# Products of ones in TensorE's planned waits, new prices and new ranks for a planned order: block-causal attention with a gated feed-forward on one core

## Chip, core and metric

The kernel runs on one core of a Trainium2 chip. The metric is the device time of one execution in microseconds (us), as a median over runs.

## What is computed

Attention over 8 batches and 8 heads (576 positions, head size 64) with a mask by blocks of 64 positions, and then a gated feed-forward layer over all 4608 rows, in fp32. The inputs of the feed-forward weights are in 64-bit floats.

```python
scores = scale * np.matmul(q, k.transpose(0, 1, 3, 2))
scores = np.where(block_i >= block_j, scores, -1000000000.0)
scores = scores - np.max(scores, axis=-1, keepdims=True)
attn = np.exp(scores)
attn = attn / (np.sum(attn, axis=-1, keepdims=True) + 1e-09)
attn_out = np.matmul(attn, v)
x = attn_out.transpose(0, 2, 1, 3).reshape(B * S, H * D)    # 4608 x 512
g = x @ w_gate                                               # 512 x 1536
val = x @ w_val
out = (g * (1.0 / (1.0 + np.exp(-g))) * val) @ w_out         # 1536 x 512
```

## The kernel before

The program first makes a list of tasks, and no task issues an instruction at that point. A task has an engine, a cost in us, a rank, a function that issues its instructions, the tasks that it waits for, and the buffers that it uses (`add`, `dma`). `in_order` (L1288) then plays the list on a clock of its own: whenever an engine is free, it takes the ready task with the lowest rank for which the buffers are free, and adds its cost. The order of the tasks that comes out is the order in which the functions are called (L1382 to L1385), and so each engine's program order. The chip then runs each engine in that order, held by semaphores alone. What a cost or rank changes is therefore the order, never the work.

The tasks are these.

- Attention goes by pairs of heads. For batches 0 and 1 (`FIRST`, stretches of 0 to 256 and 256 to 576 positions) `plain_scores` loads q and k (L387), turns them on TensorE (L411) into PSUM, copies them out with ScalarE (L419), makes the scores (L437, fp32), and ScalarE copies them to `sc` (L455) and hides the masked blocks (L469), which reads the scores' PSUM buffer last. Batches 2 to 7 split q and k into a high and a low fp32r part (`row_scores`, products L648; `split_scores`, products L564). Then VectorE takes the maximum over chunks (L705), GpSimd over partitions (L709), VectorE subtracts it (L733), ScalarE takes the exponent (L737), and TensorE multiplies with `v` (L777); in batch 0 it also multiplies with `ones` there for the sums. Later the sums are taken by TensorE (L836, L843, batch 1) or by GpSimd (L828).
- A piece of a weight (`weight`, 12 pieces of three weights) is loaded as 64-bit words (L944), brought to fp32 by ScalarE (L959, L963) and VectorE (L968, L973), and split into a high part (L978) and a low one (L981). The loads hang in one chain, and five `wo` buffers hold them. Their ranks are in `PIECES`, those of some first loads in `AHEAD`.
- The feed-forward goes by 18 tiles of 256 rows (`feed_forward`): the products with the gate and value weights into `gv` (L1100 to L1102, three fp32r products of 256 columns for each part of the depth), tanh (L1133), two operations of VectorE (L1136, L1141), the split of the result (L1146, L1149), and the products with the third weight into `po` (L1191 to L1193). Tiles 0 and 1 take their ranks from `SIDE`, later ones from their place; attention of batch b has the rank 10 + b - `LEAD`, and its scores `EAGER` less.

PSUM is held by five buffers: two `at`, two `gv` and one `po`. A task that writes one has to wait until the last reader of what stood there is done. `ones` is a 128 x 64 tile of 1.0, set by VectorE's first instruction.

Of the kernel before, what the change touches and what calls it, by code (L numbers as in the profile page):

```python
# [18 lines left out]
def kernel(  # L19
# [33 lines left out]
    LEAD, EAGER = 1.69311, 0.3  # L53
# [85 lines left out]
    class Task:  # L139
        def __init__(self, engine, cost, rank, fn, after, bufs, port, mode):  # L140
            self.engine, self.cost, self.rank, self.fn = engine, cost, rank, fn
            self.bufs, self.waits, self.next, self.ready = bufs, 0, [], 0.0
            self.moves, self.port, self.mode = 0.0, port, mode

            self.prev = None
# [3 lines left out]
    def add(engine, cost, rank, fn, after=(), bufs=(), port=False, mode=""):  # L149
# [9 lines left out]
        t.n = len(tasks)  # L159
        tasks.append(t)  # L160
        return t
# [8 lines left out]
    def mm_us(*ns):  # L170
        return sum(n / 2400.0 + 0.0145 for n in ns)
# [170 lines left out]
    def attention(R, b, h, a, e, early, bufs, lane):  # L342
# [35 lines left out]
        def plain_scores():  # L378
# [21 lines left out]
            for i in range(2):  # L400
# [24 lines left out]
                tr = add("PE", 0.083 * nb, R, transposes, [ld[i]], [qk, ps, prt])  # L425
                ready.append(add("ACT", act_us(nb * TB, True), R, out_of_psum, [tr], [ps, prt]))

            for visit in visits:
# [19 lines left out]
                for parts, ps in zip(visit, both):  # L448
# [25 lines left out]
                    if whole:  # L474
# [9 lines left out]
                        t = add("ACT", act_us(4 * BLK) + 0.1, Q, hide_there, [pr], [ps])  # L484
                        t = add("ACT", act_us(2 * W), Q, max_there, [t], [ps, mx])
# [4 lines left out]
                    if mixed:  # L490
                        t = add("ACT", 0.245 * len(mixed), Q, hide, [t], [ps, sc])
                    if parts[0][:2] == (0, 0):
                        t = add("ACT", 0.46, Q, first_max, [t], [ps, sc, mx])
# [3 lines left out]
        def split_scores():  # L497
# [48 lines left out]
            for x in range(2):  # L546
                for group in (((0, 0, half), (0, half, half)), ((1, 4), (2, 3))):
# [40 lines left out]
                    us = mm_us(*(w for _, _, w, _, _ in parts)) * 2  # L588
                    pr = add("PE", us, Q, products, ready[x], [ps, high, prt[x], sc])
# [123 lines left out]
        for c in (1, *later):  # L713
            ms.append(
                add(
                    "DVE",
                    dve_us(2 * (e - first[c])),
                    Q,
                    lambda c=c: merged(c, mx, ALU.max, scores_of),
                    [*evac[0], *evac[c], *ms[0:1], *ms[-1:]],  # L720
                    [*stays, sc, mx],
                    not stays,
                )
            )
        mm = [add("POOL", 0.1 + W * 0.0034, Q, lambda x=x: max_all(x), ms, [mx]) for x in range(2)]
# [149 lines left out]
        elif by_pe:  # L875
            tot = Buf("at", also=banks)
            sm = add("PE", pair_us(W), R, sum_all, ss, [sc, su, tot], mode="columns")
            sm = [add("ACT", act_us(W) + 0.1, R, sums_out, [sm], [tot, sr])] * 2
            total = lambda x0, x1: sr[0][x0 * D : x1 * D : D, :]
        else:  # L880
            assert (a, e) == (0, S)
            ss.append(add("ACT", act_us(2 * P), R, sum_first, [exps[0], *taken], [sc, su]))
            sm = [add("POOL", 3.82, R, lambda x=x: reduced(x), ss, [su]) for x in range(2)]
# [126 lines left out]
    def bring_x(j, t0, w):  # L1010
# [31 lines left out]
        for d in range(NDC):  # L1042
# [18 lines left out]
            m = dma(R, 2e5, r_load, [a], [rt], 2)  # L1061
# [4 lines left out]
    def feed_forward(j, t0, w, xs):  # L1066
# [19 lines left out]
        def up(i, which, prev):  # L1086
# [3 lines left out]
            for y in range(2):  # L1090

                for ds in [range(NDC)] if j >= FINE else [[d] for d in range(NDC)]:

                    def products(ds=ds, y=y):
# [11 lines left out]
                        mm_us(w, w, w) * len(ds),  # L1106
# [3 lines left out]
                        [ps, *(xs[d][1] for d in ds)],  # L1110
                    )
# [5 lines left out]
        for i in range(0, NFC, 2):  # L1117
# [65 lines left out]
            for piece in pieces:  # L1183
# [14 lines left out]
                t = add("PE", mm_us(DM, DM, DM) * len(piece), rank(i), products, after, bufs)  # L1198
# [45 lines left out]
    add("ACT", 1.4, 2.01, lambda: nc.scalar.activation(seen, seen, AF.Exp))  # L1244
# [43 lines left out]
    def in_order():  # L1288
# [4 lines left out]
        engines = ("PE", "DVE", "ACT", "POOL", "SP")  # L1293
# [4 lines left out]
        events = [0.0]  # L1298
# [32 lines left out]
        while events:  # L1331
# [3 lines left out]
            for e in engines:  # L1335
# [22 lines left out]
                if e == "PE":  # L1358
                    end, mode, last = end + 0.2 * (t.mode != mode), t.mode, t
# [21 lines left out]

    order = in_order()  # L1382
    with tc.manual_schedule():
        for t in order:
            t.fn()  # L1385
# [28 lines left out]
```

## Time and profile before

| | |
|---|---|
| median of 3 runs | 1177.16 us |
| lowest and highest run | 1176.88 and 1179.21 us |
| span of the profiled execution, first to last instruction | 1173.6 us |
| TensorE busy | 1145.5 us, 98% of the span |
| VectorE, ScalarE, GpSimd busy | 758.9, 620.4, 325.5 us |

The span is the profiled execution's own time; the median of the runs is 3.6 us above it. The page divides the span into busy time by engine; further views give the busy time in stretches, what each engine waited for, groups of instructions by line, and the instructions in order of time. TensorE's weight loads are counted apart and overlap with its products. A product's recorded end is modelled, and neighbours overlap in the record, so how long a group takes is read from the start of the next. The granted clock is given as a share of 2.4 GHz.

### The profile page before, as it was taken

The page shows a single profiled execution, that of the slowest core. Times are in us where ns is not written, and L with a number is a line of the kernel's source. Part 1 is how long each engine was busy: PE and PEld are TensorE (multiplying, and loading weights), DVE is VectorE, ACT ScalarE, POOL GpSimd, SP SyncE. Part 2 cuts the span into 40 slices and gives each one's busy share as a digit, 9 for nine tenths or more (in the row PEclk, how much of TensorE's full clock was granted, in tenths as well). Part 3 has the DMA queues.
Part 4 walks back from the last instruction along what each step waited for, and adds up shares of the span by engine and source line. Part 5 has one row for each costly group of instructions (what it writes and reads, how often), then busy time and mean ns, then how long its engine had stood idle before and what let it go on. Part 6 is the DMA issues. An engine that isn't in the chain of part 4 may idle for free.

```text
span 1173.6 us, 21780 instructions
## 1 busy us (share of the span) xinstructions
PE 1145.5 (98%) x8512; PEld 1024.7 (87%) x8512; DVE 758.9 (65%) x1230; ACT 620.4 (53%) x1114; POOL 325.5 (28%) x139
## 2 busy tenths in 40 slices
PE   5889999999999999999999999999999999999998
PEld 4568778898898989988998899898989899999997
DVE  6988988575887668768575859575767533323222
ACT  6978876546573837465656555555646312212111
POOL 3222100144535251434444334252432500000000
PEclk9989999999999999999999999999999999999999
DMA  8658756766564756656565565655663445444432
GB/s 225 188 151 219 201 187 226 206 178 166 169 148 137 198 164 167 195 166 168 152 188 160 152 177 163 187 146 161 164 202 108 145 148 197 140 167 136 143 134 100
DMA packets 266982, 197.40 MB, mean 168 GB/s; under 512 B 195264, under 2 KB 231376, under 8 KB 266880
## 3 DMA queue, kind: packets, MB, share of 16 engines
q1 hardware_dynamic: 264304, 195.29, 56.9%
q8 instruction: 67, 1.10, 0.4%
q10 hardware_dynamic: 2576, 0.72, 0.3%
q14 instruction: 35, 0.29, 0.1%
HBM read 171.57 MB, written 24.38 MB: 167 GB/s over the span
## 4 chain that ended last, share of the span: by engine, by line
PE 85%; DVE 5%; ACT 4%; DMA 3%; issue 1%; POOL 1%; SPq 1%; ACTq 0%; DVEq 0%; POOLq 0%
PE gv L1100 16%; PE gv L1102 15%; PE gv L1101 15%; PE po L1191 7%; PE po L1193 7%; PE po L1192 7%; PE at L777 7%; PE at L564 6%; DVE sc L733 1%; DVE mx L705 1%; DMA wo<-in_moe_w_val_dram 1%; POOL mx L709 1%; DMA wo<-in_moe_w_out_dram 1%; ACT ob L959 1%; PE at L648 1%
## 5 line engine op out<-in xcount | busy, mean ns | idle before, releaser
L709 POOL PARTITION_ALL_REDUCE mx<-mx x80 | 144.1, 1850 | 408.7 <-issue 135.2
L1100 PE MATMUL gv<-xhl,v_all 128*128 128x256 f32 x864 | 241.8, 280 | 0.8 <-DVE t L1136 0.7
L1102 PE MATMUL gv<-xhl,v_all 128*128 128x256 f32 x864 | 239.7, 277 | 0.0
L1101 PE MATMUL gv<-xhl,v_all 128*128 128x256 f32 x864 | 239.3, 277 | 0.0
L828 POOL PARTITION_ALL_REDUCE mx<-mx x48 | 178.9, 3775 | 201.4 <-DVE mx L705 192.8
L1136 DVE SCALAR_TENSOR_TENSOR t<-t,gv 128x512 f32<-128x512 f32 x108 | 74.0, 685 | 215.4 <-ACT t L1133 215.2
L1100 PEld LDWEIGHTS gv<-xhl,v_all 128*128 128x128 f32 x864 | 162.1, 188 | 4.9 <-issue 2.5
L1101 PEld LDWEIGHTS gv<-xhl,v_all 128*128 128x128 f32 x864 | 162.3, 188 | 0.6
L1102 PEld LDWEIGHTS gv<-xhl,v_all 128*128 128x128 f32 x864 | 162.2, 188 | 0.2
L1133 ACT ACTIVATE t<-gv 128x512 f32<-128x512 f32 x108 | 64.6, 598 | 171.2 <-PE gv L1102 171.1
L1191 PE MATMUL po<-wo,hhl 128*128 128x512 f32 x372 | 147.7, 397 | 0.0
L1192 PE MATMUL po<-wo,hhl 128*128 128x512 f32 x372 | 145.6, 391 | 0.0
L1193 PE MATMUL po<-wo,hhl 128*128 128x512 f32 x372 | 145.1, 390 | 0.2 <-DVE hhl L1149 0.2
L1146 ACT CAST hhl<-t 128x512 fp32r<-128x512 f32 x108 | 67.0, 620 | 132.1 <-DVE t L1141 129.7
L733 DVE TENSOR_TENSOR sc<-sc,mx 128x640 f32<-128x640 f32 (+6 forms) x168 | 122.7, 765 | 11.7 <-POOL mx L709 11.6
L737 ACT ACTIVATE sc<-sc 128x1024 f32<-128x1024 f32 (+3 forms) x104 | 106.0, 1029 | 45.3 <-DVE sc L733 44.9
L1100 PE MATMUL gv<-xhl,g_even 128*128 128x256 f32 x432 | 123.7, 286 | 0.0
L1102 PE MATMUL gv<-xhl,g_even 128*128 128x256 f32 x432 | 122.2, 283 | 0.4 <-DVE g_even L981 0.4
L1101 PE MATMUL gv<-xhl,g_even 128*128 128x256 f32 x432 | 122.1, 283 | 0.0
L1100 PE MATMUL gv<-xhl,g_odd 128*128 128x256 f32 x432 | 120.7, 279 | 0.0
L1101 PE MATMUL gv<-xhl,g_odd 128*128 128x256 f32 x432 | 119.6, 277 | 0.0
L1102 PE MATMUL gv<-xhl,g_odd 128*128 128x256 f32 x432 | 119.6, 277 | 0.0
(171 smaller groups left out, 2368.8 us busy)
## 6 DMA issues: line engine op xcount, KB each, us to landing
wo<-wo_d SPq DMA_DIRECT2D x200, 512.0 KB
out_dram<-ob SPq DMA_DIRECT2D x35, 256.0 KB
v<-in_v_dram SPq DMA_DIRECT2D x64, 128.0 KB
xt<-x_d SPq DMA_DIRECT2D x64, 128.0 KB
rt<-r_d SPq DMA_DIRECT2D x128, 64.0 KB
qk<-in_q_dram SPq DMA_DIRECT2D x112, 72.0 KB
qk<-in_k_dram SPq DMA_DIRECT2D x104, 72.0 KB
x_d<-xu SPq DMA_DIRECT2D x24, 288.0 KB
```

The costliest lines, as they stand in the source:

```text
L709: nc.gpsimd.partition_all_reduce(m, m, channels=P, reduce_op=bass_isa.ReduceOp.max)
L733: nc.vector.tensor_tensor(piece(c), scores_of(c), m, ALU.subtract)
L737: nc.scalar.activation(x, x, AF.Exp)
L777: nc.tensor.matmul(ps[0][own(x), 1 - i if sums else i, q0 - s0 : s1 - s0], lhsT=ones if sums else vt[0][:, 2 * lane + c, own(x)], rhs=sc[0 ...
L828: nc.gpsimd.partition_all_reduce(m, m, channels=P, reduce_op=bass_isa.ReduceOp.add)
L1100: nc.tensor.matmul(o, lhsT=hi[:, d], rhs=xhi[:, 0:w], start=first, stop=False)
L1101: nc.tensor.matmul(o, lhsT=hi[:, d], rhs=xlo[:, 0:w], start=False, stop=False)
L1102: nc.tensor.matmul(o, lhsT=lo[:, d], rhs=xhi[:, 0:w], start=False, stop=last)
L1136: nc.vector.scalar_tensor_tensor(t[0][:, 0:n], t[0][:, 0:n], 1.0, pg[0][:, 0:n], ALU.add, ALU.mult)
L1191: nc.tensor.matmul(po, lhsT=hi, rhs=whi, start=i + y == 0, stop=False)
L1192: nc.tensor.matmul(po, lhsT=hi, rhs=wlo, start=False, stop=False)
L1193: nc.tensor.matmul(po, lhsT=lo, rhs=whi, start=False, stop=i + y == NFC - 1)
```

## The change

It has four parts.

1. `keep_busy`: where the list leaves TensorE idle for over 0.3 us ahead of a task, and this task is the first user of an `at`, `gv` or `po` buffer, products of `ones` with `ones` (64 columns, into a corner of that buffer) are issued ahead of the task: one per 0.25 us of the planned gap if the task is planned before 8 us, else `FILL` (0.6) of the gap at one per 0.12 us. The task's own first product starts the buffer anew, so nothing of them is left.
2. Prices: products of the feed-forward (`up_us`, `down_us` in place of `mm_us`), a table `CHANGE` for going from one kind of product to another in place of 0.2 us, double time for TensorE before 7 us (`WARM`), GpSimd's reductions, transfers (`moves`, and 1.1 us instead of 0.9 us from the queue to the landing, 1.0 us more for `r_load`), and some small operations of ScalarE and VectorE.
3. Rules: the engines are served in another order, GpSimd takes no new task while VectorE is at a task marked `port`, and `PATIENCE` goes from 10 to 42.3 us.
4. All ranks are new: `LEAD`, `EAGER`, `AHEAD`, `LATER`, `PIECES`, `SIDE`, `FIRST`, and the lead times `spare`.

The diff without the hunks that only hand on a new price or the name of a stage:

```diff
@@ -50,7 +50,7 @@
     XT = 256
 
 
-    LEAD, EAGER = 1.69311, 0.3
+    LEAD, EAGER = 6.2781, 3.1665
 
     SUMS = 2
 
...
@@ -60,31 +60,32 @@
 
     FINE = 4
 
-    AHEAD = {(0, 1): 2.01, (0, 2): 2.07, (1, 0): 2.03, (1, 1): 2.5, (1, 2): 2.5}
-    LATER = 0.6
+    AHEAD = {(0, 1): 22.5417, (0, 2): -10.3365, (1, 0): 8.2032, (1, 1): -19.9721, (1, 2): 6.7332}
+    LATER = 2.3757
 
     PIECES = [
-        (2.46498, 1.85126, 2.0295),
-        (4.86232, 5.94853, 3.63137),
-        (4.59615, 2.52017, 1.48427),
-        (3.86967, 3.05824, 5.34888),
-        (1.93206, 3.59139, 2.41171),
-        (5.13877, 6.90631, 5.83015),
-        (3.57653, 2.93377, 2.93471),
-        (0.0797053, 1.36382, 0.915695),
-        (-2.09572, -5.85789, -4.34371),
-        (-7.47749, -5.87222, -3.82425),
-        (-7.64215, -9.14061, -8.44419),
-        (-12.1092, -9.50108, -10.8836),
+        (-6.5049, -13.4704, 10.7146),
+        (14.0963, 21.3025, 1.4141),
+        (32.0858, -0.6456, 5.5541),
+        (8.9744, 6.387, 21.8701),
+        (-12.6217, 6.2755, -24.5098),
+        (28.2796, 26.9596, 9.5596),
+        (13.4146, 37.4905, 9.0606),
+        (-36.2639, -18.6986, -5.0973),
+        (-0.5887, -7.6401, -28.1413),
+        (-6.5449, -1.352, -10.4626),
+        (-29.8841, -4.8378, -26.6713),
+        (-13.3057, -19.018, -13.6853),
     ]
 
-    SIDE = (2.97811, 4.18833)
-
-    PATIENCE = 10.0
+    SIDE = (-30.4952, 24.7881)
+
+    PATIENCE = 42.3358
+    FILL = 0.6
 
     FIRST = {
-        0: [(0, 256, (-4.21445, 2.40818, 2.05548, 2.12375)), (256, 576, (-2.9124, -2.06995, -6.61901, -4.10645))],
-        1: [(0, 256, (4.0214, 3.93624, 4.15916, 3.63076)), (256, 576, (-2.93177, 1.89587, 2.55533, 4.50202))],
+        0: [(0, 256, (-37.8906, -5.2559, -7.864, 5.3255)), (256, 576, (-14.6577, -11.0435, -35.6463, 0.7383))],
+        1: [(0, 256, (11.6297, 16.6813, 14.7013, -5.4466)), (256, 576, (-3.4185, 3.2769, 6.4793, 1.1216))],
     }
     TILES = [XT] * (NT // XT)
 
...
@@ -167,17 +168,21 @@
     def dve_us(n, one=False):
         return 0.07 + n * (0.00052 if one else 0.00104)
 
-    def mm_us(*ns):
-        return sum(n / 2400.0 + 0.0145 for n in ns)
+    def up_us(n):
+        return n * 0.1134 + (0.012 if n < 3 * NDC else 0.0)
+
+    def down_us(n):
+        return n * 0.2267
 
 
     def pair_us(*ns):
         return sum(n / 600.0 + 0.01 for n in ns)
 
-    def dma(rank, size, fn, after=(), bufs=(), n=1, engine="SP", packet=1024):
+    def dma(rank, size, fn, after=(), bufs=(), n=1, engine="SP", packet=1024, late=0.0):
 
         t = add(engine, 0.5 * n, rank, fn, after, bufs)
-        t.moves = size / packet * (9.0 + 0.0385 * packet) / 16e3
+        t.moves = size / packet * (9.5 + 0.0405 * packet) / 16e3
+        t.late = 1.1 + late
         return t
 
 
...
@@ -722,7 +727,7 @@
                     not stays,
                 )
             )
-        mm = [add("POOL", 0.1 + W * 0.0034, Q, lambda x=x: max_all(x), ms, [mx]) for x in range(2)]
+        mm = [add("POOL", 0.33 + W * 0.0028, Q, lambda x=x: max_all(x), ms, [mx]) for x in range(2)]
 
 
         exps, taken = {}, []
...
@@ -1290,20 +1296,31 @@
 
         import heapq
 
-        engines = ("PE", "DVE", "ACT", "POOL", "SP")
+        engines = ("PE", "POOL", "DVE", "ACT", "SP")
         idle = {e: 0.0 for e in engines}
         could = {e: [] for e in engines}
         room = {tag: [(0.0, i) for i in range(len(s))] for tag, s in slots.items()}
         turn = dict.fromkeys(slots, 0)
-        events = [0.0]
+        events = [0.6]
         for t in tasks:
             if not t.waits:
                 could[t.engine].append(t)
         order = []
         now = queue = 0.0
-        mode, last = "", None
-
-        spare = {"PE": 2.11536, "DVE": 0.315845, "ACT": 0.745908, "POOL": 0.0, "SP": 0.0}
+        mode, last, stage, two = "", None, "", False
+
+        WARM = 7.0
+        CHANGE = {
+            "": {"columns": 0.1, "rows": 0.2},
+            "up": {"down": 0.02, "split": 0.01, "columns": 0.13, "rows": 0.2},
+            "down": {"up": 0.072, "split": 0.01, "columns": 0.13, "rows": 0.2},
+            "split": {"up": 0.072, "down": 0.05, "columns": 0.13, "rows": 0.2},
+            "columns": {"up": 0.195, "down": 0.2, "split": 0.2, "rows": 0.19, "turn": 0.15},
+            "rows": {"up": 0.195, "down": 0.2, "split": 0.2, "columns": 0.13, "rows": 0.04, "turn": 0.15},
+            "turn": {"up": 0.04, "down": 0.04, "split": 0.04, "columns": 0.13, "rows": 0.2},
+        }
+
+        spare = {"PE": 1.9535, "DVE": 0.3392, "ACT": 0.7494, "POOL": 0.0, "SP": 0.0}
 
         def place(t, by):
 
...
@@ -1343,6 +1360,8 @@
                 )
                 if e == "DVE" and idle["POOL"] > now:
                     cand = [t for t in cand if not t.port]
+                if e == "POOL" and idle["DVE"] > now and two:
+                    continue
 
                 follow = [(now, t) for t in cand if t.prev is not None and t.prev is last]
                 if any(t.ready < now - PATIENCE for t in cand):
...
@@ -1356,13 +1375,19 @@
                 order.append(t)
                 end = now + t.cost
                 if e == "PE":
-                    end, mode, last = end + 0.2 * (t.mode != mode), t.mode, t
+                    key = t.mode or t.stage
+                    end, mode, last, stage = end + CHANGE[stage].get(key, 0.0), t.mode, t, key
+                    t.gap, t.at = now - max(idle[e], 0.6), now
+                    if now < WARM:
+                        end += end - now
+                if e == "DVE":
+                    two = t.port
                 idle[e] = end
                 heapq.heappush(events, end)
                 done = end + (0.2 if e == "PE" else 0.13)
                 if t.moves:
                     queue = max(queue, end + 0.65) + t.moves
-                    done = queue + 0.9
+                    done = queue + t.late
                 heapq.heappush(events, done)
                 for u in t.bufs:
                     u.left -= 1
...
@@ -1379,9 +1404,25 @@
         assert len(order) == len(tasks), (len(order), len(tasks), [(t.engine, t.rank, t.fn.__qualname__) for t in left][:10])
         return order
 
+    def keep_busy(t):
+        for u in t.bufs:
+            if u.tag in ("at", "gv", "po") and t is first_user[u]:
+                break
+        else:
+            return
+        to = u[0] if u.tag == "gv" else u[0][:, 0]
+        for _ in range(int(t.gap / 0.25 if t.at < 8.0 else FILL * t.gap / 0.12)):
+            nc.tensor.matmul(to[0:D, 0:D], lhsT=ones, rhs=ones, start=True, stop=True)
+
     order = in_order()
+    first_user = {}
+    for t in order:
+        for u in t.bufs:
+            first_user.setdefault(u, t)
     with tc.manual_schedule():
         for t in order:
+            if t.engine == "PE" and t.gap > 0.3:
+                keep_busy(t)
             t.fn()
 
 
```

## Rows read from the trace of the kernel before

**Rows 1.** The page, part 1: busy us (share of the span), instructions.

```profile
PE 1145.5 (98%) x8512; PEld 1024.7 (87%) x8512; DVE 758.9 (65%) x1230; ACT 620.4 (53%) x1114; POOL 325.5 (28%) x139
```

**Rows 2.** Busy time by stretch: us, busy us (instructions) of each engine, clock, DMA.

```profile
0.00:80.00 80.00, 59.29 (x462) 42.40 (x463) 64.25 (x142) 61.12 (x120) 22.44 (x26) 0.96 0.71 187
80.00:260.00 180.00, 176.70 (x1305) 147.83 (x1304) 146.16 (x249) 128.34 (x227) 36.05 (x23) 1.00 0.70 203
...
360.00:1160.00 800.00, 800.00 (x5918) 736.76 (x5917) 470.72 (x724) 367.69 (x659) 220.08 (x75) 1.00 0.54 160
1160.00:1173.60 13.60, 9.81 (x63) 8.50 (x61) 2.49 (x4) 2.18 (x4) 0.00 (x0) 0.94 0.21 75
```

**Rows 3.** TensorE's waits up to 80 us: who waited for whom, us, times, longest.

```profile
PE gv L411 <- DVE ident L316: 4.4, 1, 4.4
PE at L437 <- ACT sc L469: 3.6, 3, 1.6
PE po L437 <- ACT sc L469: 2.1, 1, 2.1
...
PE at L777 <- ACT parts L419: 1.3, 1, 1.3
PE at L437 <- DVE xt L811: 1.2, 1, 1.2
PE at L777 <- ACT sc L469: 1.1, 1, 1.1
```

**Rows 4.** Busy time by stretch, three of 10 us and one of 2 us.

```profile
10.00:20.00 10.00, 7.68 (x54) 6.09 (x54) 5.82 (x14) 8.68 (x18) 5.90 (x6) 1.00 0.95 244
20.00:30.00 10.00, 6.00 (x51) 4.15 (x51) 9.69 (x21) 7.70 (x15) 2.48 (x2) 1.00 0.86 244
30.00:40.00 10.00, 7.32 (x71) 5.18 (x67) 9.55 (x22) 9.40 (x18) 2.76 (x2) 1.00 0.66 162
...
68.00:70.00 2.00, 2.00 (x10) 0.95 (x8) 2.00 (x5) 1.57 (x4) 0.00 (x0) 0.50 0.79 210
```

**Rows 5.** The split of the weights (L981): durations ns, first and last start us.

```profile
L981 DVE TENSOR_TENSOR v_all<-wo,v_all x14: 650/685/694, 25.4 to 197.2; 128x512 fp32r<-128x512 f32 x14
```

**Rows 6.** TensorE in order of time, 55 to 74 us: start, us, operation, xcount, idle before.

```profile
55.70 2.27 PE L777 MATMUL po<-sc,v 128*64 128x320 f32 x20
57.80 2.23 PE L777 MATMUL po<-sc,ones 128*64 128x320 f32 x20
...
67.03 4.32 PE L777 MATMUL at<-sc,v 128*64 128x320 f32 x20 [1.11 <-ACT sc L469]
71.13 3.10 PE L777 MATMUL at<-sc,ones 128*64 128x320 f32 x20
```

**Rows 7.** TensorE in order of time to 21 us.

```profile
8.78 2.44 PE L411 MATMUL gv<-ident,qk 96*128 96x96 f32 x12 [0.97 <-DMA qk<-in_q_dram]
...
11.15 1.65 PE L437 MATMUL at<-parts,parts 64*128 64x256 f32 x8
12.59 1.49 PE L437 MATMUL po<-parts,parts 64*128 64x256 f32 x8
14.01 1.11 PE L411 MATMUL gv<-ident,qk 96*128 96x96 f32 x6
...
18.97 0.71 PE L411 MATMUL at<-ident,qk 96*128 96x96 f32 x6 [0.74 <-DVE sc L733]
20.43 0.92 PE L437 MATMUL at<-parts,parts 64*128 64x256 f32 x8 [0.74 <-ACT parts L419]
```

**Rows 8.** Groups of VectorE by line: busy us, mean ns of one.

```profile
L1149 DVE TENSOR_TENSOR hhl<-t,hhl 128x512 fp32r<-128x512 f32 x108 | 93.1, 862 | 40.8 <-ACT hhl L1146 40.0
L1136 DVE SCALAR_TENSOR_TENSOR t<-t,gv 128x512 f32<-128x512 f32 x108 | 74.0, 685 | 215.4 <-ACT t L1133 215.2
```

**Rows 9.** ScalarE and TensorE in order of time, around 264 us.

```profile
262.65 1.06 ACT L737 ACTIVATE sc<-sc 128x1024 f32<-128x1024 f32 x1
...
265.08 1.68 PE L777 MATMUL at<-sc,v 128*64 128x256 f32 x14
```

More of the change, by code (lines that the diff above doesn't have):

```diff
@@ L143, in __init__, with add @@
             self.moves, self.port, self.mode = 0.0, port, mode
-            self.prev = None
+            self.prev, self.stage = None, ""
     tasks = []
-    def add(engine, cost, rank, fn, after=(), bufs=(), port=False, mode=""):
+    def add(engine, cost, rank, fn, after=(), bufs=(), port=False, mode="", stage=""):
         t = Task(engine, cost, rank, fn, after, bufs, port, mode)
@@ L158, in add @@
             u.left += 1
-        t.n = len(tasks)
+        t.n, t.stage = len(tasks), stage
         tasks.append(t)
@@ L423, in out_of_psum @@
                     )
-                tr = add("PE", 0.083 * nb, R, transposes, [ld[i]], [qk, ps, prt])
+                tr = add("PE", 0.083 * nb, R, transposes, [ld[i]], [qk, ps, prt], stage="turn")
                 ready.append(add("ACT", act_us(nb * TB, True), R, out_of_psum, [tr], [ps, prt]))
@@ L482, in max_there @@
                             nc.scalar.copy(mx[0][:, :, L + P : L + W], ps[0][:, :, P:W])
-                        t = add("ACT", act_us(4 * BLK) + 0.1, Q, hide_there, [pr], [ps])
-                        t = add("ACT", act_us(2 * W), Q, max_there, [t], [ps, mx])
+                        t = add("ACT", act_us(4 * BLK) + 0.03, Q, hide_there, [pr], [ps])
+                        t = add("ACT", act_us(2 * (W - P), True), Q, max_there, [t], [ps, mx])
                         evac[0].append(t)
@@ L490, in plain_scores @@
                     if mixed:
-                        t = add("ACT", 0.245 * len(mixed), Q, hide, [t], [ps, sc])
+                        t = add("ACT", 0.16 + 0.107 * len(mixed), Q, hide, [t], [ps, sc])
                     if parts[0][:2] == (0, 0):
-                        t = add("ACT", 0.46, Q, first_max, [t], [ps, sc, mx])
+                        t = add("ACT", 0.3, Q, first_max, [t], [ps, sc, mx])
                     for c, _, _ in parts:
@@ L586, in hide @@
                             )
-                    us = mm_us(*(w for _, _, w, _, _ in parts)) * 2
-                    pr = add("PE", us, Q, products, ready[x], [ps, high, prt[x], sc])
+                    us = 0.523 if len(parts) == 2 else 1.123
+                    pr = add("PE", us, Q, products, ready[x], [ps, high, prt[x], sc], stage="split")
                     t = add("ACT", act_us(2 * gw, True), Q, out_of_psum, [pr], [ps, sc])
@@ L716, in attention @@
                     "DVE",
-                    dve_us(2 * (e - first[c])),
+                    dve_us(2 * (e - first[c])) + (dve_us(2 * P) if stays else 0.0),
                     Q,
@@ L877, in attention @@
             sm = add("PE", pair_us(W), R, sum_all, ss, [sc, su, tot], mode="columns")
-            sm = [add("ACT", act_us(W) + 0.1, R, sums_out, [sm], [tot, sr])] * 2
+            sm = [add("ACT", act_us(W, True), R, sums_out, [sm], [tot, sr])] * 2
             total = lambda x0, x1: sr[0][x0 * D : x1 * D : D, :]
@@ L882, in attention @@
             ss.append(add("ACT", act_us(2 * P), R, sum_first, [exps[0], *taken], [sc, su]))
-            sm = [add("POOL", 3.82, R, lambda x=x: reduced(x), ss, [su]) for x in range(2)]
+            sm = [add("POOL", 3.5, R, lambda x=x: reduced(x), ss, [su]) for x in range(2)]
             total = lambda x0, x1: su[0][0:1, x0, :]
@@ L1060, in bring_x @@
             l = dma(R, 2e5, load, l, [xt])
-            m = dma(R, 2e5, r_load, [a], [rt], 2)
+            m = dma(R, 2e5, r_load, [a], [rt], 2, late=1.0)
             l = add("DVE", dve_us(w), R, divide, [l, m], [xt, rt], True)
@@ L1105, in up @@
                         "PE",
-                        mm_us(w, w, w) * len(ds),
+                        up_us(3 * len(ds)),
                         rank(i),
@@ L1110, in up @@
                         [ps, *(xs[d][1] for d in ds)],
+                        stage="up",
                     )
@@ L1197, in feed_forward @@
                 bufs = [*dict.fromkeys(accs[m] for _, m in piece), hh, *(took[y][1] for y in ys if took[y][1])]
-                t = add("PE", mm_us(DM, DM, DM) * len(piece), rank(i), products, after, bufs)
+                t = add("PE", down_us(3 * len(piece)), rank(i), products, after, bufs, stage="down")
                 for m in ms:
@@ L1241, in with_v @@
         at_work.clear()
-    add("ACT", 1.4, 2.01, lambda: nc.scalar.activation(seen, seen, AF.Exp))
+    add("ACT", 0.4, 2.01, lambda: nc.scalar.activation(seen, seen, AF.Exp))
     for b in range(B):
```

## Prediction

> **What bounds the kernel now.** I read the page first, for the engine that has no room. TensorE is busy for 1145.5 us of a span of 1173.6 us [rows 1], so 28.1 us of its time are idle. Then the busy time by stretches [rows 2], to see where those 28.1 us lie: 20.7 us in the first 80 us, 3.3 us from 80 to 260 us, nothing from 360 to 1160 us, and 3.8 us at the end, where the last result is copied out and stored (0.3 us is left for the stretch between). The work of TensorE in the long stretch is the same products in any order, so it is a queue of fixed length: a microsecond that the start gains or loses arrives at the end unchanged. I therefore work the sum out in TensorE's time, and nearly all of it in the first 80 us.
>
> Third, the waits of TensorE in that stretch [rows 3]. 4.4 us is the wait of the first transpose for `ident`. Of the other 16 us most are waits for a PSUM buffer, not for data: the score products at L437 read only what L419 has written, so where L437 waits for L469, it waits until L469 has read the old scores out of the buffer; and L777, which reads only `sc` and `v`, waits for L419 in the same way. Adding L437 <- L469 (3.6 and 2.1), L777 <- L469 (1.1), L777 <- L419 (1.3) and L437 <- L811 (1.2, the buffer that the division of tile 0 reads) gives 9.3 us. The releasers are ScalarE and VectorE, and they have no room there: from 20 to 40 us VectorE is busy for 9.69 and 9.55 of each 10 us, and ScalarE for 7.70 and 9.40 [rows 4]. They carry the attention of two batches and, in between, the splitting of the weights, which goes on to 197 us [rows 5].
>
> Fourth, TensorE's clock. The granted clock is 0.50 from 68 to 70 us [rows 4], the lower of the two levels (1.2 GHz; 2.4 GHz is the other), and the group that ran into it began at 67.03 us after a wait of 1.11 us [rows 6]. At the very start the clock column says 1.00, but the durations say the lower level: eight L437 products took 1.65 us at 11.15 us and 0.92 us at 20.43 us [rows 7].
>
> **The change, part by part.** It adds products of ones, changes the prices and rules by which the list is planned, and gives nearly every rank a new value. Everything is an order of the same tasks; no transfer or product of the computation is added or removed.
>
> *Products at the start.* In the list the first transposes wait some microseconds for `q` and `k`, and the added products (one per 0.25 us of gap) run there. They cost nothing on TensorE, which waited 4.44 us anyway; what they may give is the clock. The cold groups from 8.78 us on, priced at full speed from the same shapes later [rows 7]: twelve transposes 2.44 us against 2 x 0.71 = 1.42; eight L437 1.65 against 0.92; eight L437 into `po` 1.49 against 0.92; six transposes 1.11 against 0.71. That is 6.69 against 3.97, a gain of at most 2.7 us. Work behind it waits for ScalarE's copies in part, so I take 2.0, with 0 and 2.7 as ends. TensorE: Matmul & The Clock Gate in the Trainium skill (section "What's actually happening") says that the throttled clock is the default and activity releases it. The slow rows agree; by that rule the sum would take the whole 2.7.
>
> *The dip.* Twice twenty L777 products took 4.32 and 3.10 us in it against 2.27 and 2.23 us at full clock [rows 6], 2.9 us too much. If products of ones keep the clock up, that is the gain; if the new order has a dip of its own, it is 0. I take 1.5, the middle.
>
> *Products in later waits.* They write into the buffer that the following task is the first to use, and in TensorE's rows each group starts behind the one before it. If the buffer has long been free, they fill idle time. If the wait is for the buffer, they start only when it is released, and then stand ahead of the real product. The price of one: twenty L777 instructions (two for each product, five chunks of 320, 320, 320, 192 and 64 columns, two heads at once: 1216 columns) start 2.10 us before the next group [rows 6], 1.73 ns a column, so 64 columns take an estimated 0.11 us. FILL/0.12 = 5 products per us of planned gap then lengthen such a gap by 0.55 of itself: with the 9.3 us of buffer waits above, 5.1 us at most, 0 at least. I take 2.0: the list plans shorter gaps if its prices are better, and ScalarE and VectorE have queues that absorb some of the delay. PSUM — Partial Sum Buffer in the Trainium skill (section "Engine vs sequencer instructions") says that matmuls start and complete in program order. That rule speaks against the change; by it alone this term is the full 5.1 us, which is the first rival below.
>
> *Prices.* The old list has a group of 12 products of the first matmul at 12 x (256/2400 + 0.0145) = 1.45 us, the new one at 1.36: a list whose TensorE is 6% slower there than the new one's. It had a flat 0.2 us for a change from one kind of product to another, now a table. The mean duration of L1149 is 862 ns against 685 of L1136 with the same number of elements [rows 8]: the one reads two operands out of SBUF, the other one of them out of PSUM, and the difference fits a wait for GpSimd. The new rule that GpSimd doesn't start beside such an operation plans for this. I book the prices at 0 by themselves; they work through the order.
>
> *The order.* 20.7 - 4.4 = 16.3 us of idle time remain in the first 80 us [rows 2]. With the same total of work on ScalarE (61.1 of 80 us) and VectorE (64.3 of 80) there is room, 16 to 19 us on each, but little of it from 20 to 40 us [rows 4], where 6.7 of the 16.3 us lie. What a new order can do is to move the splitting of weights (L968, L973, L981 and ScalarE's part) out from between the score tasks, or to give TensorE products of tile 0 to do in a wait. Tile 0 gets the rank -30.5 and tile 1 24.8, pieces of the weights go as far back as 37.5, and the attention moves ahead by LEAD and EAGER. I see no way to read the new idle time from this trace, so I bound it: a gain of 14 us at best (2 us of waits left), a loss of 10 us at worst (a third more waits in 80 us and a few more to 260 us). I take a gain of 6.5 us, four tenths of the 16.3, since about six tenths of the waits go with a ScalarE and a VectorE that are full in any order. Past 260 us I take 0: the products L777 of batch 2 start at 265.08 us, 1.4 us after the exponent's end at 263.71 us [rows 9], so attention already goes as fast as its own chain, and LEAD = 6.3 can't pull it far; TensorE has the feed-forward to fill in.
>
> *Sum.* -2.0 - 1.5 + 2.0 - 6.5 = -8.0 us. In the profiled execution's own time 1173.6 becomes 1165.6 us. The median of the runs shown is 3.6 us above that span, which I carry over: 1177.2 - 8.0 = 1169.2 us, 0.7% faster.
>
> **The rivals.**
> 1. *The products stand in the way (slower).* Mechanism: the wait is for PSUM's release in nearly every gap, so products run after the release. The price is 5.1 us on TensorE, less 2.0 for the start, with nothing from dip and order, since each delay comes back through ScalarE: 1177.2 + 3.1 = 1180.3 us. It decides once the products' delay is over what clock and order give, so where dip and order together give under 3.1 us. For it: 9.3 of 16.3 us are buffer waits. Against: the products are planned for six tenths of a gap, and in the new order the gaps may be others.
> 2. *TensorE runs out of feed-forward work.* Pieces of weights with ranks of 14 to 37 stand behind the attention of later batches on VectorE and ScalarE; they are needed by tile 0, and the loads hang in one chain on five buffers. In the trace, the last piece of the second weight is split at 197 us [rows 5] and TensorE has only 3.3 us of idle time from 80 to 260 us [rows 2]. If the last pieces come 20 us later and attention covers half of that, TensorE idles for 10 us: 1187 us.
> 3. *The waits are ScalarE's and VectorE's anyway.* The order changes which product waits, not for how long; clock and products about cancel: -2 us, 1175 us. For it: VectorE at 96% from 20 to 40 us [rows 4].
> 4. *The order fills nearly all.* 14 us instead of 6.5 with the other terms as they are: 1161.7 us. For it: the flat 0.2 us and the 6% made the list's waits others than the chip's, and each wait that the new list places right is one that work can be put into.
>
> **How the numbers follow.** Forecast (1169 us) 0.45; rival 1 (1180) 0.15; rival 2 (1187) 0.11; rival 3 (1175) 0.17; rival 4 (1162) 0.12. The likeliest is the forecast. A measurement of this kernel can tell about 0.2%, 2.4 us. Faster by more than that, under 1174.8 us: forecast, rival 4 and a third of rival 3, 0.63. Within 0.2%: most of the rest of rival 3 and the low edge of rival 1, 0.14. Slower: 0.23. The range leaves out the lower half of rival 4 and most of rival 2: 1160 to 1184 us.
>
> **What would show it.** In the profile of the changed kernel: a line of TensorE products on `ones` into `gv`, `at` and `po`, most of them before 80 us; the first L437 group at about 0.9 us instead of 1.65; no stretch of granted clock 0.5 before 100 us; and in the stretches, TensorE idle (counting the products of ones as idle) at about 10 us instead of 16.3 between the first transpose and 80 us, with 40.00 of 40 us busy later. If the products of ones start where ScalarE's read of the same buffer ends, rival 1 is at work. If TensorE idles between 80 and 260 us behind L981, it is rival 2. The prediction is wrong in its base if TensorE idles after 360 us, since then the work isn't a queue of fixed length.

## The result: 0.44% slower

| | median, us | range | runs |
|---|---|---|---|
| before | 1177.02 | 1174.91 to 1179.21 | 6 |
| with the change | 1181.76 | 1180.66 to 1184.12 | 6 |

The ratio is 1.0044 with an interval of 1.0033 to 1.0055: 4.7 us slower, where 8.0 us faster was forecast. The profiled execution has a span of 1178.7 us, against 1173.6 us.

The code has moved by a few lines: L416 is the old L411 (transposes), L424 L419, L442 L437 (scores), L474 L469, L782 L777, L816 L811. L1415 is the line of the added products.

Busy time of the changed kernel by stretch, with the columns of [rows 2], and then of L1415 alone (TensorE's products, then its weight loads):

```profile
0.00:80.00 80.00, 63.97 (x583) 50.32 (x585) 58.00 (x128) 55.83 (x108) 18.69 (x24) 0.96 0.67 175
80.00:260.00 180.00, 176.99 (x1353) 148.05 (x1351) 153.51 (x265) 135.12 (x240) 35.60 (x25) 1.00 0.69 197
360.00:1160.00 800.00, 800.00 (x5952) 737.71 (x5951) 464.92 (x727) 371.54 (x662) 224.79 (x76) 1.00 0.54 162
```

```profile
0.00:8.00 8.00, 4.37 (x36) 3.99 (x36) 1.00 0.74 182
8.00:80.00 72.00, 14.24 (x158) 12.54 (x158) 0.95 0.66 175
80.00:260.00 180.00, 1.47 (x18) 1.20 (x18) 1.00 0.69 197
```

TensorE is idle for 16.0 us instead of 20.7 in the first 80 us, and looks better used. But 18.6 of its 64.0 busy us are products of ones. Counted as the prediction wanted it, with the products of ones as idle, TensorE is idle for 30.0 us from its first transpose (4.59 us) to 80 us, where about 10 were forecast. Without the 194 records of ones (each product of ones leaves two) it has executed 583 - 194 = 389 products by 80 us, where the kernel before had 462, and at 260 us 1724 against 1767 [rows 2]: 43 behind. At 180 us for 1305 products (0.138 us each) that is 5.9 us, which is about the whole loss. (Of the 73 that are missing at 80 us, 26 are the new order's own and are made up later: e1 below, the same order without products of ones, has 436 by 80 us and 1763 by 260 us.) From 360 to 1160 us TensorE is busy for 800.00 of 800 us in both. So the base of the prediction held: what the start loses arrives at the end.

The added products in TensorE's waits (columns as in [rows 3]):

```profile
PE po L1415 <- ACT sc L474: 5.0, 3, 2.1
PE at L1415 <- DVE xt L816: 4.2, 1, 4.2
PE at L1415 <- ACT parts L424: 3.1, 3, 1.6
PE at L1415 <- ACT sc L474: 1.6, 1, 1.6
PE po L416 <- ACT sc L474: 1.2, 1, 1.2
```

and in order of time, with what ended the idle time ahead of them:

```profile
20.93 3.15 PE L1415 MATMUL at<-ones 128*64 128x64 f32 x28 [4.23 <-DVE xt L816]
24.01 0.55 PE L416 MATMUL at<-ident,qk 96*128 96x96 f32 x4
...
31.31 1.15 PE L1415 MATMUL po<-ones 128*64 128x64 f32 x16 [1.76 <-ACT sc L474]
32.38 0.98 PE L442 MATMUL po<-parts,parts 64*128 64x320 f32 x8
...
76.32 1.15 PE L1415 MATMUL at<-ones 128*64 128x64 f32 x16 [1.62 <-ACT sc L474]
77.39 0.81 PE L442 MATMUL at<-parts,parts 64*128 64x320 f32 x4
```

This is rival 1 to the letter. L1415 reads nothing but `ones`, yet it waits for L816, L474 and L424, the last readers of the buffer that it writes. When they are done, the scores or transposes behind it could start; instead 28 records of ones run for 3.08 us (20.93 to 24.01, at the lower clock level, into which TensorE fell in the wait ahead of them), and 16 for 1.07 us. Nine groups from 20 to 93 us begin after such a wait; the waits sum to 14.8 us, and the groups take 10.3 us.

### The profile page after: what moved, and what is told of

It reads as the page before. It is cut to its first block, busy times and chain, and to the rows that moved or that the text cites. A ratio compares the mean times of both kernels' runs of the same rounds, so it can differ in the third digit from the quotient of the medians.

```text
span 1178.7 us, 22269 instructions
## 1 busy us (share of the span) xinstructions
PE 1155.5 (98%) x8724; PEld 1039.0 (88%) x8724; DVE 747.1 (63%) x1230; ACT 624.3 (53%) x1114; POOL 323.1 (27%) x139
## 4 chain that ended last, share of the span: by engine, by line
PE 88%; ACT 4%; DMA 3%; DVE 2%; issue 1%; SPq 1%; POOL 0%; ACTq 0%; DVEq 0%; POOLq 0%
PE gv L1105 16%; PE gv L1107 16%; PE gv L1106 16%; PE po L1197 8%; PE po L1198 7%; PE po L1199 7%; PE at L782 7%; PE at L569 5%; DMA wo<-in_moe_w_val_dram 2%; PE at L653 1%; ACT sc L460 1%; DVE mx L710 1%; PE at L1197 1%; PE at L1198 1%; PE at L1199 1%
## 5 line engine op out<-in xcount | busy, mean ns | idle before, releaser
L1155 DVE TENSOR_TENSOR hhl<-t,hhl 128x512 fp32r<-128x512 f32 x108 | 90.4, 838 | 112.4 <-ACT hhl L1152 109.0
L1105 PE MATMUL gv<-xhl,g_odd 128*128 128x256 f32 x432 | 120.5, 279 | 0.0
L1107 PE MATMUL gv<-xhl,g_odd 128*128 128x256 f32 x432 | 119.4, 276 | 0.0
```

Of the source, the lines that this page charges most:

```text
L1105: nc.tensor.matmul(o, lhsT=hi[:, d], rhs=xhi[:, 0:w], start=first, stop=False)
L1107: nc.tensor.matmul(o, lhsT=lo[:, d], rhs=xhi[:, 0:w], start=False, stop=last)
L1155: nc.vector.tensor_tensor(hh[1][:, 0:n], t[0][:, 0:n], hh[0][:, 0:n].bitcast(F32), ALU.subtract)
```

## The experiments

Times are medians; ratios are against runs of the kernel before on the same chip, with 95% intervals. The kernel before had medians of 1176.6 to 1177.1 us in the four sets of runs.

| | median, us | ratio to before | interval |
|---|---|---|---|
| the change | 1181.76 | 1.0044 | 1.0033 to 1.0055 |
| e1_no_ones | 1174.83 | 0.9981 | 0.9971 to 0.9991 |
| e2_start_only | 1176.49 | 0.9996 | 0.9988 to 1.0005 |
| e3_after_release | 1175.90 | 0.9987 | 0.9976 to 0.9998 |
| e4_double | 1189.99 | 1.0103 | 1.0086 to 1.0121 |
| e5_before_products | 1177.43 | 1.0006 | 0.9993 to 1.0019 |
| e6_before_start | 1177.53 | 1.0008 | 0.9995 to 1.0021 |
| e7_old_ranks_new_prices | 1184.61 | 1.0069 | 1.0050 to 1.0089 |
| e8_new_ranks_old_prices | 1191.20 | 1.0128 | 1.0109 to 1.0146 |
| e9_free_buffer | 1173.29 | 0.9973 | 0.9963 to 0.9983 |
| e10_free_late | 1172.10 | 0.9963 | 0.9952 to 0.9973 |
| e11_before_free | 1174.19 | 0.9981 | 0.9971 to 0.9992 |

### Products or order? (e1, e2, e3, e4)

Theory A is that the products stand behind a release and in front of the real work; theory B, that the new order is slower by itself. Four kernels keep the change's order and vary the products.

e1_no_ones:

```diff
-        for _ in range(int(t.gap / 0.25 if t.at < 8.0 else FILL * t.gap / 0.12)):
+        for _ in range(0):
```

> The changed kernel without any product of ones; prices, rules, ranks and so the order are those of the change. Theory A (the products run after the release of the buffer that they write, and so stand in front of the real product): those from 20 us on take 11.2 us of TensorE's time in the changed kernel, so this kernel comes 8 to 11 us below it, at 1171 to 1174 us, less whatever a colder clock costs. Theory B (the new order is slower by itself and the products fill idle time): no gain, 1180 to 1184 us.

1174.83 us: 6.9 us below the change and a little below the kernel before. The order isn't at fault; with it alone the kernel is 0.2% faster, and theory B falls. It lies 0.8 us above A's range, in which the cost of a colder clock was left out. Two stretches of e1 and two of the changed kernel (the last three numbers are granted clock, DMA share and GB/s):

```profile
22.00:26.00 4.00, 3.92 (x22) 2.70 (x22) 3.15 (x6) 2.66 (x5) 1.17 (x2) 0.50 0.58 136
46.00:50.00 4.00, 4.00 (x20) 2.71 (x20) 4.00 (x8) 3.64 (x8) 0.00 (x0) 0.50 0.74 200
```

```profile
20.00:24.00 4.00, 3.08 (x28) 3.01 (x28) 4.00 (x9) 1.75 (x3) 2.74 (x3) 0.57 0.47 139
37.00:41.00 4.00, 3.61 (x24) 2.65 (x24) 2.82 (x6) 3.68 (x8) 1.00 (x1) 0.57 0.78 195
```

Without products the new order falls to half clock in its waits: in e1 the record has 17.1 us of it before 100 us, in the changed kernel 6.8 us. The kernel before has 6.8 us too, in the one stretch of [rows 4]. So the late products do what they are for, and still cost more than they bring.

e2_start_only:

```diff
-        for _ in range(int(t.gap / 0.25 if t.at < 8.0 else FILL * t.gap / 0.12)):
+        for _ in range(int(t.gap / 0.25 if t.at < 8.0 else 0)):
```

> The changed kernel with the products of ones only ahead of tasks planned before 8 us (two groups, 18 products). Theory A: as the kernel without products, and 1 to 3 us better by the clock at the start: 1169 to 1173 us. Theory B: 1180 us or more.

1176.49 us, above e1 and not below it: theory A's expectation for the late products held, the one for the start didn't. The clock rose and was lost again: the first scores, at 6.40 us, take 0.92 us instead of 1.65, but then TensorE waits 3.49 us for `q`, the granted clock is 0.50 from 10.8 to 17.5 us, and the second scores, at 13.18 us, take 1.65 us as in e1.

e3_after_release counts a gap only from the time at which the list has the buffer free:

```diff
+                if tag in ("at", "gv", "po"):
+                    t.free = max(t.free, f[0])
...
-                    t.gap, t.at = now - max(idle[e], 0.6), now
+                    t.gap, t.at = now - max(idle[e], 0.6, t.free), now
```

> The changed kernel with the gap ahead of a task counted only from the moment at which, in the list, its PSUM buffer is free. In the list nearly all gaps after 12 us are waits for the buffer, so only three groups remain, all before 12 us. Theory A: 1169 to 1173 us; against the kernel with the start alone this tells what the third group, 15 products ahead of the transposes at 8 to 11 us, is worth: within 1 us. Theory B: 1180 us or more.

1175.90 us, against an expectation of 1169 to 1173. Its list of gaps shows more than its time: of the groups that the change issues after 12 us none remains, that is, in the list too all these gaps last until the buffer's release, to within the 0.3 us below which no products are issued. The fault could be read off the list itself. What the start does is seen by laying e1 (first two lines) and e3 (last two) side by side:

```profile
17.96 0.82 PE L782 MATMUL at<-sc,ones 128*64 128x256 f32 x8
21.35 2.17 PE L416 MATMUL at<-ident,qk 96*128 96x96 f32 x10 [2.57 <-DVE xt L816]
```

```profile
16.23 0.85 PE L782 MATMUL at<-sc,ones 128*64 128x256 f32 x8
22.16 2.17 PE L416 MATMUL at<-ident,qk 96*128 96x96 f32 x10 [5.08 <-DVE xt L816]
```

With the warm clock TensorE is 1.7 us ahead at 16 us. Then it waits 2.5 us longer for VectorE's division (L816), and starts 0.8 us later than without. The start's clock buys a longer wait. What holds VectorE there is a piece of a weight: L973, which stands ahead of the division in its order, waits for ScalarE's L964, and that for the piece's landing. In e1 (first line) L964 started without a wait, in e3 (the other two) nearly 2 us later:

```profile
15.66 0.78 ACT L964 ACTIVATE ob<-wo 128x512 f16<-128x512 f32 x1
17.52 0.78 ACT L964 ACTIVATE ob<-wo 128x512 f16<-128x512 f32 x1 [2.10 <-DMA wo<-in_moe_w_val_dram]
18.32 0.69 DVE L973 SCALAR_TENSOR_TENSOR wo<-wo,ob 128x512 int32<-128x512 int32 x1 [3.30 <-ACT ob L964]
```

A faster TensorE doesn't bring that landing forward. Why it came later in e3 isn't shown; the execution in this trace, 1178.53 us, is the longest of e3's twelve.

e4_double:

```diff
-    FILL = 0.6
+    FILL = 1.2
```

> The changed kernel with FILL = 1.2, so twice the products after 8 us. Theory A: what the products take after 8 us, 14.4 us, is doubled, less what a wait of another cause absorbs: 8 to 14 us slower, 1190 to 1196 us. Theory B: the products fill idle time, so little changes, 1181 to 1185 us.

1189.99 us, 8.2 us above the change, as theory A had it at its low end. From 0.6 of a gap to 1.2 the products cost 8.2 us, from the start alone (e2) to 0.6 they cost 5.3.

### The wait or the products? (e9, e10)

If the release is the fault, the same products in a buffer that nobody holds must be harmless. e9 asks the list for a PSUM buffer that has been free for over 0.3 us when the task is planned (after 12 us always a `gv`, which tile 0 uses seldom then), counts the gap from there, and writes there; a task need no longer be the first user of a buffer:

```diff
+                    free = [(f, tag) for tag in ("gv", "at", "po") for f in room[tag] if f[0] < now - 0.3]
+                    if free:
+                        f, tag = min(free)
+                        t.fill = tag, f[1]
+                        t.gap = now - max(idle[e], 0.6, f[0])
...
-        to = u[0] if u.tag == "gv" else u[0][:, 0]
+        tag, place = t.fill
+        to = tiles_of(tag, place)[0]
+        to = to if tag == "gv" else to[:, 0]
```

> The changed kernel, same order, with about the same products of ones, but written into a PSUM buffer that is free in the list all through the gap (nearly always gv, which tile 0 uses seldom then), so that they need not wait for the buffer of the task behind them. Theory A (the wait for the release is the fault, not the products): they run in the idle time; the 11 us behind releases go, the clock stays up: 1170 to 1175 us, and TensorE's products on ones start right behind the group before them. Rival (products delay whatever stands behind them, in any buffer, since the chip's gaps are shorter than the list's): 1178 to 1182 us.

1173.29 us, 8.5 us below the change with the same order and 228 records of ones instead of 212. This settles the cause: it is the buffer that they write, not the products. One mark of the expectation failed for the largest group, whose `gv` was free in the list and not yet on the chip:

```profile
15.76 0.85 PE L782 MATMUL at<-sc,ones 128*64 128x256 f32 x8
20.22 3.10 PE L1417 MATMUL gv<-ones 128*64 128x64 f32 x28 [3.61 <-ACT parts L424]
23.26 0.81 PE L416 MATMUL at<-ident,qk 96*128 96x96 f32 x4
```

It waited for L424 and ran at half clock (3.4 us in e9, the only stretch). It still cost 0.2 us at most: L816, for which the transposes behind it wait, ended at 23.08 us (22.67 + 0.41). The other groups after 12 us start right behind the group before them.

e10_free_late leaves out those before 12.5 us:

```diff
-        for _ in range(int(t.gap / 0.25 if t.at < 8.0 else FILL * t.gap / 0.12)):
+        for _ in range(int(0 if t.at < 12.5 else FILL * t.gap / 0.12)):
```

> As the kernel with free buffers, but without the products before 12.5 us, of which two kernels showed that they gain nothing. Theory A: 1170 to 1174.5 us, at or below the kernel without products (1174.8), by what half clock it still had after 20 us. Rival: 1176 us or more.

1172.10 us, 0.37% below the kernel before and 0.8% below the change: the best version here. Its products (L1417) in order of time:

```profile
18.12 0.82 PE L782 MATMUL at<-sc,ones 128*64 128x256 f32 x8
18.77 1.79 PE L1417 MATMUL gv<-ones 128*64 128x64 f32 x28
21.42 0.55 PE L416 MATMUL at<-ident,qk 96*128 96x96 f32 x4 [0.85 <-DVE xt L816]
...
26.91 1.15 PE L1417 MATMUL gv<-ones 128*64 128x64 f32 x16
28.81 0.98 PE L442 MATMUL po<-parts,parts 64*128 64x320 f32 x8 [0.76 <-ACT sc L474]
```

The same 28 records now run inside the wait, and TensorE still waits 0.85 us for L816 after them: they delay nothing. The clock stays up; two of its stretches, which take in the first two in which e1 is at half clock:

```profile
20.00:28.00 8.00, 7.14 (x75) 5.42 (x73) 7.90 (x19) 6.79 (x12) 2.95 (x4) 1.00 0.78 201
44.00:52.00 8.00, 8.00 (x73) 5.36 (x72) 7.34 (x16) 5.52 (x13) 2.77 (x2) 1.00 0.97 252
```

### The same products in the order of before (e5, e6, e11)

e5 puts the change's `keep_busy` into the kernel before, with nothing else:

```diff
+                    t.gap, t.at = now - max(idle[e], 0.6), now
...
+            if t.engine == "PE" and t.gap > 0.3:
+                keep_busy(t)
```

> The kernel before with its own ranks, prices and rules, so its own order, and the change's products of ones alone (at the start and for six tenths of a later gap). Its list has 18 gaps over 0.3 us, and 13 of those after 12 us end at the very moment at which the PSUM buffer is released. Theory A (a product behind a release costs what it takes): about 65 products of 0.13 us after 12 us are 8 to 9 us, less 3 us for the stretch at half clock that they prevent and 0 to 2 us at the start: 1180 to 1184 us. Theory B (products are harmless, the order of the change was at fault): 1172 to 1177 us.

1177.43 us, no difference beyond the noise: it lies 0.4 us above theory B's range, and theory A missed. The products after 8 us do take 12.1 us of TensorE there, most of them run behind a release as well, and the record has as much half clock as before (6.8 us, now in two stretches from 16 to 27 us). Why they cost so little isn't shown. Idle time in the first 80 us goes from 20.7 to 11.2 us, but that isn't the reason: in the profiled execution, 1179.38 us and the longest of the ten, TensorE has executed 627 - 192 = 435 products of the computation by 80 us and 1734 by 260 us, 27 and 33 fewer than before, so in this execution they did cost. One possible reason is that a product behind a release costs what it takes only where TensorE is on the chain. The chain of work that ended last, in the first 100 us, as shares of that window, of the kernel before (first), of e1 and of the change points that way:

```profile
by line: PE at L777 7.2%; POOL mx L709 6.3%; DMA wo<-in_moe_w_val_dram 5.5%; ACT sc L455 5.4%; issue 5.3%; ACT sc L737 5.1%; ACT ob L959 5.0%; DVE sc L733 4.6%; PE at L437 4.4%; PE po L777 4.3%; DVE mx L705 3.2%; ACT wo L963 3.2%; DMA qk<-i
```

```profile
by line: PE at L782 15.1%; ACT sc L460 7.5%; DMA qk<-in_k_dram 7.1%; PE at L442 4.9%; issue 4.4%; PE po L442 4.4%; DMA qk<-in_q_dram 4.2%; DVE sc L738 3.7%; ACT ob L964 3.4%; PE at L416 3.3%; ACT sc L742 3.2%; PE gv L1105 2.8%; ACT parts L4
```

```profile
by line: DMA wo<-in_moe_w_val_dram 9.4%; ACT sc L460 8.3%; PE at L782 7.6%; DMA qk<-in_k_dram 7.4%; PE at L1415 7.3%; PE po L782 6.4%; PE po L1415 4.7%; ACT sc L742 4.6%; ACT ob L964 4.3%; PE at L416 3.6%; issue 3.2%; SPq L392 2.8%; PE at L
```

Summing its pieces by engine, TensorE has 22.7 us of the window's chain before and 38.6 us in e1, and GpSimd 6.3 us before and nothing in e1; in the change 12.1 us of the chain are L1415 itself. The new order would then run closer along TensorE, with less behind which a delay can hide. That is a reading of one chain in one execution each, not a test, and the record gives no chain of e5 in this window.

e6 has only the products at the start:

```diff
-        for _ in range(int(t.gap / 0.25 if t.at < 8.0 else FILL * t.gap / 0.12)):
+        for _ in range(int(t.gap / 0.25 if t.at < 8.0 else 0)):
```

> The kernel before with products of ones only ahead of tasks that its list places before 8 us. Theory of the prediction (a clock raised at the start is worth 2.0 us): 1174 to 1175.5 us. Rival (ScalarE, VectorE and transfers hold the start anyway): 1176 to 1178 us.

1177.53 us, inside the rival's range. But it tests neither side: the clock wasn't up behind these products. The second scores of e6 and its products with `ones` (first two lines) take as long as at the lower level, where the kernel before (last line) had already left it:

```profile
11.85 1.65 PE L438 MATMUL at<-parts,parts 64*128 64x256 f32 x8
18.71 1.52 PE L778 MATMUL at<-sc,ones 128*64 128x256 f32 x8
17.38 0.85 PE L777 MATMUL at<-sc,ones 128*64 128x256 f32 x8
```

e11 has the late ones, in free buffers as in e10 (the same edit in the kernel before):

> The kernel before, own order, prices and rules, with products of ones after 12.5 us in buffers that are free in its list. Theory A: no release is waited for, the stretch at half clock at 66 to 73 us goes: 1173 to 1176 us. Rival (clock isn't what holds this order; VectorE and ScalarE are): 1176 to 1178 us.

1174.19 us, 0.19% faster, with no stretch at half clock after 15 us. The stretch at 66 to 73 us [rows 4, 6] was worth about the 2.9 us that the prediction read from its rows, of which it took half.

### Ranks or prices? (e7, e8)

e7 is e1 with the old ranks:

```diff
-    LEAD, EAGER = 6.2781, 3.1665
+    LEAD, EAGER = 1.69311, 0.3
...
-    SIDE = (-30.4952, 24.7881)
+    SIDE = (2.97811, 4.18833)
```

(and so on through `AHEAD`, `LATER`, `PIECES`, `PATIENCE`, `FIRST` and `spare`)

> The changed kernel without products of ones and with the ranks, PATIENCE and lead times of the kernel before; prices and rules are the new ones. If the 2 us that the new order gains come from the prices and rules, this is at 1174 to 1176 us as well; if from the ranks, at 1177 us or above, since the old ranks were not chosen for these prices.

e8 is the kernel before with the new ones, the same lines the other way round:

> The kernel before with the new ranks, PATIENCE and lead times, and its old prices and rules; no products of ones. If the ranks alone carry the gain: 1174 to 1176 us. If ranks only fit the prices for which they were chosen: 1178 to 1186 us, with more waits in the first 120 us.

1184.61 and 1191.20 us, 0.7% and 1.3% slower than before; together (e1) they are 0.2% faster. Neither half has a gain of its own; prices and rules weren't taken apart. Both kernels are also at half clock for longer before 100 us (23.9 and 30.7 us, against 6.8 before), so a part of their loss may be the clock's. For e8, the expected 1178 to 1186 was still too kind. Its stretches (columns as in [rows 2]):

```profile
0.00:80.00 80.00, 58.16 (x393) 40.26 (x395) 63.45 (x137) 61.05 (x115) 19.59 (x24) 0.89 0.72 189
80.00:260.00 180.00, 170.72 (x1243) 138.36 (x1240) 144.53 (x242) 123.81 (x224) 36.35 (x25) 0.97 0.66 188
```

393 products by 80 us instead of 462, and 9.3 us idle from 80 to 260 us instead of 3.3 [rows 2]. Ranks are priorities within one list; with other prices they make another list, and here they didn't transfer.

## Why the prediction was wrong

The runs split the change into the prediction's own terms, each from a pair of kernels. The first pair of each row forms a chain from the kernel before over e1, e10 and e9 to the change, so that their sum is the whole by construction; the pairs in brackets are apart from it. Each difference is uncertain by over 1 us (the intervals above reach 1.2 us to either side for most kernels), and two of them, e10 against e1 and the change against e9, are between different sets of runs.

| term | predicted, us | measured, us | from |
|---|---|---|---|
| order, prices, rules | -6.5 | -2.3 | e1 against before (with the clock kept up: e10 against e11, -2.1) |
| clock in later waits | -1.5 | -2.7 | e10 against e1 (in the old order: e11 against before, -2.6) |
| products at the start | -2.0 | +1.2 | e9 against e10 (e3 against e1, +1.1; with the clock not kept up: e2 against e1, +1.7, and e6 against before, +0.9) |
| products behind a release | +2.0 | +8.5 | the change against e9 |
| sum | -8.0 | +4.7 | |

- **Products behind a release.** The mechanism was named, as rival 1, with the right mark in the trace, and was given 0.15. The step that failed most is "I take 2.0" for these products, 6.5 us off, and its upper bound of 5.1 us was too low as well: the products ran behind the release in nearly every gap and cost 8.5 us of the 10.3 that they take. (A little of the 8.5 is clock: 6.8 us at half clock in the change, 3.4 in e9.) Three things made it so. The bound counted 9.3 us of such waits from the old order; in the new one they sum to 14.8 us, 4.23 of it for L816 alone. A product took 0.134 us (16 records, 8 products, in 1.07 us) and not the estimated 0.11, and 0.22 us in the group at half clock. And the step argued that ScalarE's and VectorE's queues absorb part of the delay: in the old order the products cost little in all (e5), in the new one they cost nearly what they take. The argument that waits for a PSUM buffer were 9.3 of 16.3 us [rows 3] was already enough to make this the likeliest case: a product that writes the buffer whose release is awaited can't run in the wait, whatever the order. "Against: the gaps may be others" was no reason, since the list makes gaps for the same cause.
- **The order.** This is the second step that failed, 4.2 us off. The 6.5 us was four tenths of the idle time, taken with no row for it, and the text said so. With the order alone, TensorE is idle in the first 80 us for as long as before (20.7 us in e1), as rival 3 had it, and it gains 2.3 us. What rival 3 and the step shared, that ScalarE and VectorE are full there [rows 4], should have weighed more.
- **The start.** The step took it that products ahead of the first transposes raise the clock for the groups behind them and that this gain arrives at the end. Already the first half was unsure: in the change the first scores, at 6.53 us, still take 1.65 us, in e2 the clock fell again, and in e6 it didn't rise. Where it was up from 11 us on (the second scores in e3 take 0.92 us instead of 1.65, as the later rows of [rows 7] said they could; e9 is alike), there was no gain either. It was counted on TensorE's work and not on what is late next: VectorE's division, behind a piece of a weight, for which e3 waits 2.5 us longer. The cost is 1.1 and 1.2 us in the two pairs with the clock up, each near the edge of its interval, so that it gains nothing in this order is better shown than that it costs. In the old order it wasn't tested.
- **The clock later.** Right in kind, and the size was above what was taken (2.9 was the upper end).
- **Right:** the queue of fixed length after 360 us; that the attention's lead moves nothing past 260 us (0.55 us of idle time from there to 360 us); that TensorE doesn't run out of feed-forward work (rival 2: 176.99 of 180 us from 80 to 260 us against 176.70). Not right was the mark of no half clock before 100 us: there were two stretches of it, each about 3.4 us.

Rival 1's time, 1180.3 us, lies 1.5 us below the measured one. That is near in part by luck: its sum had the products' price 3.4 us too low and a start of -2.0 that isn't there, and left out the 5.0 us that the order and the clock gave.

## What to carry to other kernels

An instruction put into a wait runs in it only if it doesn't wait for the same thing: a filler needs a buffer that is free at the start of the gap, and written into the buffer of the work behind it, it lands on the far side of the release. Before trusting idle time that has become busy, count the real work done by a given time: here TensorE's idle time fell by 4.7 us in the stretch in which it got 73 products behind. A count is safest against a kernel with the same order: against e1 it is 47. Ranks chosen under one set of prices were worth nothing under another here: the halves of the pair cost 8.0 and 14.6 us, the pair gained 2.3.

## What the runs showed of the hardware

- TensorE went to the lower of its two clock levels within the waits of the first 100 us in every version without late products (17.1 us at 0.50 in e1, 6.8 us in the kernel before), and not at all after 20 us with 80 products of 64 columns in the gaps (e10). Keeping it up was worth 2.6 us in the old order and 2.7 in the new, 0.2% of the kernel. At the start of e2 the scores behind 36 records of ones took 0.92 us instead of 1.65, and after a wait of 3.49 us the next ones took 1.65 again.
- PSUM — Partial Sum Buffer in the Trainium skill (section "Engine vs sequencer instructions") says that matmuls start and complete in program order. The rows agree: at 20.93 us L416, whose buffer had just come free, started 3.08 us later, after the products ahead of it.
